# A scan-plus-MLP kernel on one core: a wider on-chip turn, weights decoded in place, and MLP2's weights decoded late

## The chip, the cores and the metric

The kernel runs on one core of a Trainium2 chip. Its time is the device time of one launch in microseconds (us). The kernel before has a median of 1177.3 us in 3 runs (1176.42 to 1181.52).

## What is computed

Three stages on 4 batches of 768 tokens, 8 heads of 40 features (320 in all):

```python
# 1. per head, over t = 0..767: a 40x40 state
y[t] = r[t] @ state
state = state * w[t][:, None] - outer(state @ a[t], b[t]) + outer(v[t], k[t])
# 2. x = y as [768, 320]; token mixing, then a first MLP
h = relu(x.T @ w_tok1) @ w_tok2          # 768 -> 256 -> 768
u = x + h.T
x = u + relu(u @ w_ch1) @ w_ch2          # MLP1: 320 -> 1536 -> 320
# 3. layer norm and a second MLP
out = x + relu(norm(x, g_ln) @ d_ch1) @ d_ch2   # MLP2: 320 -> 1280 -> 320
```

The MLP weights come as 64-bit floats. Every product runs as three f16 matmuls on a high and a low half of each operand.

## The kernel before, in words

**Scan.** Time is cut into chunks of 64 steps, 12 for each batch, 48 in all, taken in 24 pairs. The inputs r, k, v, w, a, b are prepared in six groups G of 8 chunks: `stack` (L778) multiplies an input by running products of w, splits it into f16 halves in the tile `o16` and stores it to a DRAM scratch (`scr_a`, `scr_b`, ...). Later loads read the scratch back, some turned by the DMA. For groups 0 and 1, a and b are also turned on the chip: `turn` (L814) multiplies 32-row slices of `o16` with an identity, 128 matmuls for each input, and ScalarE and VectorE in turn copy eight PSUM banks out (L831, L829). b goes for that time into `d2`, the tile that is later MLP2's second weight. Then come `gram` (L846), and `solve` (L866), 30 dependent steps of two VectorE operations on the tile `ug` (L878, L880), whose result goes to DRAM (`t_d`) and is read by `early` (L996). After that `chain` (L1034) runs each chunk, in order, and `yout_a`, `yout_b` write a batch's x to DRAM (`x_d`).

**Weights.** `decode` (L1150) loads a piece of a weight (up to 384 numbers wide) into a tile `raw`, and four VectorE operations turn the 64-bit floats into 32-bit ones in another tile `wst` (L1155 to L1162). `split` (L1176) scales on ScalarE (L1177), makes the high half on ScalarE (L1180) and the low half on VectorE (L1181). There are 56 pieces: 34 of t1, t2, c1, c1t, c2 and 22 of d1, d1t, d2 (MLP2's weights). `raw` and `wst` are in a pool `boot` that is closed before the pool `moe`, which holds everything of the MLPs, can open in the same memory.

**MLPs.** For each batch, `token_load` reads six tiles xt; `token1` (L1236) makes the hidden token layer in two halves of 160 features, `token2` (L1250) adds the result to xt. `mlp1` (L1319) and `mlp2` (L1330) then work on blocks of 256 tokens, three of each for a batch. In `mlp` (L1296) every 128x512 result is split by ScalarE (L1264) and VectorE (L1265) before the second matmul.

**Order of the work.** All of that is traced in one program order (L1400 to L1440). Then `fix_order` (L543) lists each engine's instructions anew: it plays the program with a table of costs (`cost`, L200) and fixes the order that came out shortest, for PE, DVE, ACT, POOL and the DMA queue on SP. Each engine then runs its list strictly in order, so an instruction that waits holds all behind it. Pools with several buffers add waits: a load into a buffer waits for the last reader of what was there.

Of the kernel before, what the change touches and what calls it, by code (L numbers as in the profile page):

```python
# [200 lines left out]
def cost(i, engine):  # L201
# [351 lines left out]
def tile_main(  # L553
# [47 lines left out]
    WCOL = 384  # L601
# [80 lines left out]
    NA = 8  # L682
# [126 lines left out]
    def t_steps(G):  # L809
# [4 lines left out]
        def turn(n):  # L814
            for i in range(4):
                st = st_i.setdefault(i, {})
                if n == "a":
                    st[n] = stk.tile([128, TU * 128], F16, name="at", bufs=NA)
                    st_t.setdefault(4 * G + i, {})["a"] = st[n]
                else:  # L820
                    st[n] = wt["d2"].rearrange("p m l c -> p (m l c)")[:, i * TU * 128:(i + 1) * TU * 128]
                ls = slice(32 * i, 32 * i + 32)
                for t0 in (0, 16):
                    pt = ps_b.tile([128, 512], F32, name="pb", tag="b")[0:120].rearrange("p (l t) -> p l t", t=16)
                    for t in range(16):
                        nc.tensor.matmul(pt[:, :, t], o16[ls, t0 + t, 0:120], ident[ls, ls], start=True, stop=True)  # L826
                    dst = st[n][0:120].rearrange("p (l t) -> p l t", t=HC)[:, :, t0:t0 + 16]
                    if t0:
                        V.tensor_copy(dst, pt)  # L829
                    else:  # L830
                        A.activation(out=dst, in_=pt, func=ACTF.Copy)  # L831

        def gram_load(i):
            r0 = i * TU * 128
            st = st_i[i] = {}
            st["a"] = stk.tile([128, TU * 128], F16, name="at", bufs=NA)
# [313 lines left out]
    def decode(src, pieces, n):  # L1150
# [4 lines left out]
        V.scalar_tensor_tensor(out=bits[:, 0:n], in0=raw[:, 0:n, 1], scalar=0x38000000, in1=bits[:, 0:n],  # L1155
                               op0=ALU.bitwise_xor, op1=ALU.bitwise_or)
        f = boot.tile([128, WCOL], I32, name="wst", bufs=3)
        V.tensor_scalar(out=f[:, 0:n], in0=raw[:, 0:n, 1], scalar1=0x07FFFFFF, scalar2=3,
                        op0=ALU.bitwise_and, op1=ALU.logical_shift_left)
        nc.vector.scalar_tensor_tensor(out=f[:, 0:n], in0=raw[:, 0:n, 1], scalar=-0x40000000, in1=f[:, 0:n],  # L1160
                                       op0=ALU.bitwise_and, op1=ALU.bitwise_or)
        nc.vector.scalar_tensor_tensor(out=f[:, 0:n], in0=raw[:, 0:n, 0], scalar=29, in1=f[:, 0:n],  # L1162
                                       op0=ALU.logical_shift_right, op1=ALU.bitwise_or)
        return f[:, 0:n].bitcast(F32)
# [3 lines left out]
    def weight_steps():  # L1168
        steps = []

        def cols_of(cols, fn):
            n = cols // -(-cols // WCOL)
            for c0 in range(0, cols, n):
                steps.append(lambda c0=c0: fn(c0, n))

        def split(f, s, hi, lo, p0=0):  # L1176
            A.activation(out=f, in_=f, func=ACTF.Copy, scale=s)  # L1177
            if len(hi.shape) > 2:
                f = by_head(f)
# [3 lines left out]
        def full(name, cols, src, nk, e, gs=None, out=lambda x: x):  # L1183
# [3 lines left out]
            def one(i, c0, n):  # L1187
                f = decode(src, [(0, i * 128, 128, c0)], n)
# [3 lines left out]
            for i in range(nk):  # L1192
                cols_of(cols, lambda c0, n, i=i: one(i, c0, n))
# [293 lines left out]
```

## Time and profile before

| | |
|---|---|
| median of 3 runs | 1177.3 us (1176.42 to 1181.52) |
| profiled execution: time / span | 1180.47 / 1178.8 us |
| PE busy / DVE busy / ACT busy / POOL busy | 904.6 / 770.8 / 507.4 / 206.3 us |
| granted TensorE clock, mean | 0.979 |
| DMA queue of SP | 159.04 MB, 66.6% of 16 engines' span |

PE is TensorE's matmuls, DVE is VectorE, ACT is ScalarE, POOL is GpSimd, SP issues the DMAs. Busy time of an engine is the time in which at least one of its instructions ran; matmuls are pipelined, so their records overlap and the mean of one is longer than the pace at which they follow each other.

### The profile page before, as it was taken

Reading aid. Unit: us, or ns where it says so; the run is one execution under the profiler, and the core shown is the slowest. Engines: PE = TensorE matmul, PEld = TensorE weight load, DVE = VectorE, ACT = ScalarE, POOL = GpSimd, SP = SyncE. Lnnn points to the kernel's source line nnn. Section 1 sums busy time; section 2 is a strip of 40 time slices with the busy share of each in tenths; the row PEclk is TensorE's granted clock in tenths of the full one; section 3 lists DMA queues with packets and bytes.
Section 4 is the critical chain, followed back from the end, with each engine's and each line's share of the span. In section 5 each row is a group of like instructions: output and inputs, shape, how many; then the busy total and the mean of one; then the engine's idle time right before and its main releaser. Section 6 shows DMA issues by size and latency. Waiting matters only on the chain.

```text
span 1178.8 us, 39814 instructions
## 1 busy us (share of the span) xinstructions
PE 904.6 (77%) x17422; PEld 734.4 (62%) x17422; DVE 770.8 (65%) x1936; ACT 507.4 (43%) x1105; POOL 206.3 (17%) x212
## 2 busy tenths in 40 slices
PE   0631450155588878899899999898999999999996
PEld 0620440154577756677677777676777888787774
DVE  6679485868977695657865689656964563443432
ACT  1443333455655453554445545554553343332221
POOL 0235450332000631034120052201000000000000
PEclk9999999999999989989999999999999999999998
DMA  5569826879998778958999757897565532221111
GB/s 159 155 171 242 189 72 193 260 146 182 229 190 162 179 157 198 186 102 160 154 204 162 166 118 170 144 174 173 111 115 93 80 47 47 52 44 21 36 17 26
DMA packets 356903, 161.67 MB, mean 137 GB/s; under 512 B 327536, under 2 KB 336752, under 8 KB 353136
## 3 DMA queue, kind: packets, MB, share of 16 engines
q1 hardware_dynamic: 356720, 159.04, 66.6%
q8 instruction: 138, 2.26, 0.8%
q14 instruction: 45, 0.37, 0.1%
HBM read 71.70 MB, written 50.59 MB: 104 GB/s over the span
## 4 chain that ended last, share of the span: by engine, by line
PE 34%; DVE 8%; DMA 4%; ACT 2%; issue 1%; SPq 1%; POOL 0%; DVEq 0%; ACTq 0%
PE pb L1317 12%; PE pa L1307 9%; PE ch L935 4%; PE pa L1310 3%; PE ps L935 3%; DVE ug L880 1%; DVE hh L1265 1%; PE ps L1014 1%; PE ps L1258 1%; DMA xt<-x_d 1%; DVE tmp L878 1%; DVE u L890 1%; PE ps L993 1%; DMA x<-in_v_dram 1%; DMA x<-in_r_dram 1%
## 5 line engine op out<-in xcount | busy, mean ns | idle before, releaser
L1317 PE MATMUL pb<-c,hh 128*128 128x320 f16 x864 | 179.5, 305 | 2.8 <-ACT hh L1264 2.1
L1317 PEld LDWEIGHTS <-hh 128*128 128x128 f16 x1584 | 153.4, 99 | 39.1 <-ACT hh L1264 3.0
L1265 DVE SCALAR_TENSOR_TENSOR hh<-pa,hh 128x512 f16<-128x512 f32 x132 | 90.6, 687 | 125.8 <-ACT hh L1264 125.3
L1307 PE MATMUL pa<-ut,c 128*128 128x256 f16 x864 | 159.4, 275 | 4.8 <-issue 2.4
L1264 ACT ACTIVATE hh<-pa 128x512 f16<-128x512 f32 x132 | 78.5, 595 | 173.0 <-PE pa L1310 168.2
L1317 PE MATMUL pb<-d,hh 128*128 128x320 f16 x720 | 147.6, 301 | 0.9 <-ACT hh L1264 0.7
L1307 PE MATMUL pa<-ut,d 128*128 128x256 f16 x720 | 137.7, 279 | 9.1 <-DVE hh L1265 6.2
L1307 PEld LDWEIGHTS <-c 128*128 128x128 f16 x864 | 83.4, 99 | 25.7 <-issue 5.3
L1307 PEld LDWEIGHTS <-d 128*128 128x128 f16 x720 | 69.8, 100 | 25.8 <-issue 8.2
L795 ACT ACTIVATE o<-x 128x2560 f16<-128x2560 f32 x30 | 69.9, 2331 | 20.9 <-DMA x<-in_a_dram 7.2
L880 DVE TENSOR_TENSOR ug<-ug,tmp 128x30 f32<-128x30 f32 (+9 forms) x180 | 73.0, 405 | 1.4
L878 DVE TENSOR_TENSOR tmp<-ug 128x30 f32<-128x30 f32 (+9 forms) x180 | 69.5, 386 | 4.2 <-POOL ug L872 2.6
L1343 POOL TENSOR_TENSOR y<-ve,mhalf 128x2 f32<-128x2 f32 x12 | 8.9, 741 | 353.3 <-DVE stats L1339 214.6
L826 PE MATMUL pb<-ident,o 32*120 32x32 f16 x512 | 50.3, 283 | 23.8 <-POOL o L797 13.2
L1310 PE MATMUL pa<-ut,c1t 128*128 128x256 f16 x288 | 65.4, 276 | 0.0
L826 PEld LDWEIGHTS <-o 32*120 32x120 f16 x512 | 49.1, 214 | 24.7 <-POOL o L797 13.4
L797 POOL TENSOR_TENSOR o<-x,o 128x1280 f16<-128x1280 f32 x15 | 49.7, 3314 | 59.2 <-ACT o L795 40.3
L935 PEld LDWEIGHTS <-srx 64*64 64x64 f16 x2304 | 51.8, 122 | 10.8 <-issue 8.1
L1310 PE MATMUL pa<-ut,d1t 128*128 128x256 f16 x240 | 55.5, 277 | 0.0
L858 PE MATMUL pa<-at,d 120*32 120x32 f16 (+1 forms) x384 | 5.2, 206 | 63.9 <-DVE lc L862 61.3
L935 PE MATMUL ch<-vx,sak 64*64 64x40 f16 x1152 | 33.9, 198 | 26.4 <-DVE n L1087 16.7
L722 POOL TENSOR_TENSOR x<-x,sx 128x1280 f32<-128x1280 f32 x10 | 33.1, 3307 | 115.7 <-DMA x<-in_k_dram 63.5
(204 smaller groups left out, 1914.2 us busy)
## 6 DMA issues: line engine op xcount, KB each, us to landing
raw<-in_moe_w_ch_dram SPq DMA_DIRECT2D x30, 320.0 KB
scr_b<-o SPq DMA_DIRECT2D x6, 1024.0 KB
scr_k<-o SPq DMA_DIRECT2D x6, 1024.0 KB
scr_v<-o SPq DMA_DIRECT2D x6, 1024.0 KB
scr_r<-o SPq DMA_DIRECT2D x6, 1024.0 KB
t_d<-u SPq DMA_DIRECT2D x24, 256.0 KB
tu<-t_d SPq DMA_DIRECT2D x24, 256.0 KB
scr_a<-o SPq DMA_DIRECT2D x4, 1024.0 KB
```

Of the source, the lines that this page charges most:

```text
L722: eng.tensor_tensor(out=o, in0=x, in1=y, op=ALU.mult)
L795: A.activation(out=hi2, in_=x.unsqueeze(2).broadcast_to([128, HC, 2, D]), func=ACTF.Copy, scale=p2(e))
L797: P.tensor_tensor(out=o16[:, :, lo:lo + D], in0=x, in1=o16[:, :, 0:D], op=ALU.subtract)
L826: nc.tensor.matmul(pt[:, :, t], o16[ls, t0 + t, 0:120], ident[ls, ls], start=True, stop=True)
L878: V.tensor_tensor(out=tv, in0=ug[:, 0:s, s:s + 1].broadcast_to([128, s, n]), in1=ug[:, s:s + 1, s + 1:32].broadcast_to([128, s, n]), op=AL ...
L880: V.tensor_tensor(out=ug[:, 0:s, s + 1:32], in0=ug[:, 0:s, s + 1:32], in1=tv, op=ALU.add)
L935: m = nc.tensor.matmul(out, lhsT, rhs, start=start, stop=stop, skip_group_check=True)
L1264: nc.scalar.activation(out=hi, in_=ps, func=ACTF.Relu)
L1265: nc.vector.scalar_tensor_tensor(out=lo, in0=ps, scalar=0.0, in1=hi, op0=ALU.max, op1=ALU.subtract)
L1307: nc.tensor.matmul(o, w1[:, f, l, ms], ut[:, f + 3 * q, :], start=n == 0, stop=False)
L1310: nc.tensor.matmul(o, w1t[:, ms], ut[:, 2 + 3 * q, :], start=False, stop=q == 1)
L1317: nc.tensor.matmul(pb[i][:, 0:DM], hh[:, l, c0:c0 + 128], w2[:, m0 + s, q, :], start=m0 + s == 0 and n == 0, stop=m0 + s == nm - 1 and n == 2)
```

## The change

Five edits, and the engines' orders that follow from them:

1. `turn` works on all 128 rows of `o16` at once: 32 matmuls of 128x128 (32 pieces of time, output step 4 floats) for an input in place of 128 of 32x32 (output step 16 floats). Still eight banks are copied out.
2. `decode` works in place in `raw` (four buffers, no `wst`), with the same number of VectorE operations; `split` puts the scale into the two operations that make the halves, so ScalarE's separate scaling goes. Tiles whose columns are regrouped by head (c2, d2) are split in two halves.
3. d1, d1t and d2 are no longer decoded before `moe` opens but traced after it (`run(wlate)`), 160 numbers wide in 44 pieces in place of 22, in four tiles borrowed from the rings xt and xn of `moe`.
4. The token layer of batch 0 is made in one walk (`wide`) of full 320 columns, in both `pa` banks.
5. Batch 0 runs its three MLP1 blocks, then MLP2 (before: MLP1 0, MLP1 1, MLP2 0, MLP1 2, MLP2 1). The planner's cost for a PE output with a step is at least 100 ns.

```diff
 def cost(i, engine):
+        if i.outs[0].ap[-1][0] > 1:
+            return max(100, t), 0
 def turn(n):
-                ls = slice(32 * i, 32 * i + 32)
-                for t0 in (0, 16):
-                    for t in range(16):
-                        nc.tensor.matmul(pt[:, :, t], o16[ls, t0 + t, 0:120], ident[ls, ls], start=True, stop=True)
+            for t0 in range(0, HC, 4):
+                pt = ps_b.tile([128, 512], F32, name="pb", tag="b")[0:120].rearrange("p (l t) -> p l t", t=4)
+                for t in range(4):
+                    nc.tensor.matmul(pt[:, :, t], o16[:, t0 + t, 0:120], ident, start=True, stop=True)
+                if t0 % 8:
+                    V.tensor_copy(dst[:, :, t0:t0 + 4], pt)
+                else:
+                    A.activation(out=dst[:, :, t0:t0 + 4], in_=pt, func=ACTF.Copy)
 def decode(src, pieces, n, raw=None):
-        raw = boot.tile([128, WCOL, 2], I32, name="raw", bufs=3)
+        if raw is None:
+            raw = boot.tile([128, WCOL, 2], I32, name="raw", bufs=4)
...
-        f = boot.tile([128, WCOL], I32, name="wst", bufs=3)
+        lo, hi = raw[:, 0:n, 0], raw[:, 0:n, 1]
+        V.tensor_scalar(out=lo, in0=lo, scalar1=29, scalar2=-0x40000000,
+                        op0=ALU.logical_shift_right, op1=ALU.bitwise_xor)
+        V.scalar_tensor_tensor(out=lo, in0=hi, scalar=3, in1=lo,
+                               op0=ALU.logical_shift_left, op1=ALU.bitwise_xor)
+        V.scalar_tensor_tensor(out=lo, in0=hi, scalar=-0x80000000, in1=lo,
+                               op0=ALU.bitwise_and, op1=ALU.bitwise_or)
+        def slot():
+            if not slots_d:
+                for name in ("xt", "xt", "xn", "xn"):
+                    t = moe.tile([128, DM], F32, name=name, bufs=8 if name == "xt" else 2)
+                    slots_d.append(t.bitcast(I32).rearrange("p (c w) -> p c w", w=2))
+            slots_d.append(slots_d.pop(0))
+            return slots_d[-1]
 def split(f, s, hi, lo, p0=0):
-            A.activation(out=f, in_=f, func=ACTF.Copy, scale=s)
...
-            A.activation(out=hi, in_=f, func=ACTF.Copy)
-            V.tensor_tensor(out=lo, in0=f[p0:128], in1=hi[p0:128], op=ALU.subtract)
+            A.activation(out=hi, in_=f, func=ACTF.Copy, scale=s)
+            V.scalar_tensor_tensor(out=lo, in0=f[p0:128], scalar=s if isinstance(s, float) else s[p0:128],
+                                   in1=hi[p0:128], op0=ALU.mult, op1=ALU.subtract)
+    def wide(bb):
+        ps = [token_bank(bb) for _ in range(NJ)]
+        for i in range(NT):
...
+                    nc.tensor.matmul(ps[jt][:, 0:DM], wt["t1"][:, i, l, jt * 128:(jt + 1) * 128], o[:, m, :],
+                                     start=i == 0 and n == 0, stop=i == NT - 1 and n == 2)
 def moe_body(bb):
+        if bb == 0:
+            return ([lambda k=k: mlp1(bb, k) for k in range(NBK)]
+                    + [lambda k=k: mlp2(bb, k) for k in range(NBK - 1)])
...
     run(wtodo)
     late.close()
     moe = late.enter_context(tc.tile_pool(name="moe", bufs=2))
+    attend(0, 4)
+    run(bg(2))
+    attend(4, 8)
+    run(wlate)
```

Three places of the engines' lists that the steps below use. The first is DVE at the turn of b of group 1, beside the solve of group 0 (`ug` and `tmp` are the solve's, `d2_181` takes the turned b, `pb` are its PSUM banks, `raw`, `wst`, `bits` belong to the decoding of weights). Before:

```order
L829 CAST d2_181<-pb_1006 120x32x16
L878 TENSOR_TENSOR tmp_841<-ug_829 128x84
L829 CAST d2_181<-pb_1042 120x32x16
L880 TENSOR_TENSOR ug_829<-ug_829,tmp_841 128x3x28
L1160 SCALAR_TENSOR_TENSOR wst_1864<-raw_1860,wst_1864 128x384
L878 TENSOR_TENSOR tmp_844<-ug_829 128x108
L829 CAST d2_181<-pb_1078 120x32x16
```

Now:

```order
L831 CAST d2_181<-pb_799 120x128x4
L1198 SCALAR_TENSOR_TENSOR c1t_170<-raw_1430,c1t_170 64x384
L831 CAST d2_181<-pb_811 120x128x4
L882 TENSOR_TENSOR tmp_640<-ug_634 128x30
L1167 SCALAR_TENSOR_TENSOR raw_1439<-raw_1439 128x384
L831 CAST d2_181<-pb_823 120x128x4
```

The copies of the turn still stand among the solve's steps and the decoding; the solve now begins between them.

The second is DVE at the start of batch 0's first MLP1 block (`hh` are the splits of its hidden layer; `xn_6516`, `xn_6515` and the like are now borrowed tiles with late weights). Before:

```order
L878 TENSOR_TENSOR tmp_4893<-ug_4803 128x58
L1265 SCALAR_TENSOR_TENSOR hh_7824<-pa_7807,hh_7824 128x512
L880 TENSOR_TENSOR ug_4803<-ug_4803,tmp_4893 128x29x2
L878 TENSOR_TENSOR tmp_4896<-ug_4803 128x30
L880 TENSOR_TENSOR ug_4803<-ug_4803,tmp_4896 128x30
L1265 SCALAR_TENSOR_TENSOR hh_7856<-pa_7839,hh_7856 128x512
```

Now:

```order
L1306 SCALAR_TENSOR_TENSOR hh_7466<-pa_7449,hh_7466 128x512
L884 TENSOR_TENSOR ug_4139<-ug_4139,tmp_4172 128x10x21
L1194 SCALAR_TENSOR_TENSOR d2_181<-xn_6516,d2_181 128x80
L882 TENSOR_TENSOR tmp_4175<-ug_4139 128x220
L1306 SCALAR_TENSOR_TENSOR hh_7498<-pa_7481,hh_7498 128x512
L884 TENSOR_TENSOR ug_4139<-ug_4139,tmp_4175 128x11x20
L1194 SCALAR_TENSOR_TENSOR d2_181<-xn_6516,d2_181 128x80
L882 TENSOR_TENSOR tmp_4178<-ug_4139 128x228
L1163 TENSOR_SCALAR xn_6515<-xn_6515 128x160
```

The block's splits, which stood beside the last steps of the solve of group 2, now stand beside its middle, with late weights between.

The third is SP while the chains of batch 0 run (`kt`, `vt`, `rt`, `kb`, `yw`, `tu` are loads for the chains, `raw`, then `xt` and `xn` with `in_moe_w_ch`, are weights). Before:

```order
L957 DMA kb<-scr_b_129 128x8x80
L966 DMA yw<-scr_y_132 128x8x40
L1146 DMA x_d_3062<-yo 64x2x160 x2
L1153 DMA raw<-in_moe_w_ch_dram 128x640 x2
L957 DMA vx<-scr_v_130 128x8x80
L864 DMA l_d_141<-sab 128x8x32
```

Now:

```order
L958 DMA_TRANSPOSE kt<-scr_k_128 128x1024
L1257 DMA xt<-x_d_2401 128x320
L1158 DMA xt<-in_moe_w_ch_dram 64x320 x2
L1158 DMA xn<-in_moe_w_ch_dram 64x320 x2
L1158 DMA xt<-in_moe_w_ch_dram 64x320 x2
L958 DMA_TRANSPOSE rt<-scr_r_131 128x1024
```

The weight loads in this stretch are narrower and more of them stand between the loads for the chains.

## Rows read from the trace of the kernel before

**Rows 1.** The page: span, and busy time of each engine.
```profile
span 1178.8 us, 39814 instructions
PE 904.6 (77%) x17422; PEld 734.4 (62%) x17422; DVE 770.8 (65%) x1936; ACT 507.4 (43%) x1105; POOL 206.3 (17%) x212
```

**Rows 2.** Stretches of the span: busy time by engine, clock, DMA share, GB/s.
```profile
0.00:198.00 198.00, 60.79 (x932) 58.36 (x933) 134.01 (x304) 67.28 (x114) 68.02 (x79) 1.00 0.64 164
...
198.00:441.00 243.00, 154.01 (x4099) 130.69 (x4099) 197.93 (x476) 132.81 (x303) 57.85 (x45) 0.99 0.92 192
441.00:470.00 29.00, 25.87 (x329) 19.81 (x327) 16.04 (x42) 11.60 (x22) 5.28 (x8) 0.94 0.86 189
470.00:612.00 142.00, 128.24 (x2591) 98.77 (x2590) 98.43 (x253) 69.68 (x147) 35.97 (x40) 0.93 0.93 160
612.00:1179.00 567.00, 535.65 (x9478) 426.75 (x9476) 324.43 (x865) 225.98 (x520) 39.15 (x40) 0.98 0.51 96
```

**Rows 3.** Timeline of DVE: solve of group 0, first step and end, its stall.
```profile
120.99 0.19 DVE L878 TENSOR_TENSOR tmp<-ug 128x30 f32<-128x30 f32 x1 [2.63 <-POOL ug L872]
...
189.71 0.33 DVE L1158 TENSOR_SCALAR wst<-raw 128x320 int32<-128x320 int32 x1 [13.75 <-DMA raw<-in_moe_w_ch_dram]
...
198.27 0.20 DVE L880 TENSOR_TENSOR ug<-ug,tmp 128x30 f32<-128x30 f32 x1
```

**Rows 4.** What DVE waited for, 0 to 200: total, times, longest.
```profile
DVE wst L1158 <- DMA raw<-in_moe_w_ch_dram: 25.1, 6, 13.7
DVE d L829 <- PE pb L826: 14.9, 8, 3.1
DVE at L829 <- PE pb L826: 7.0, 5, 2.0
```

**Rows 5.** Timeline of PE: one turn of a; four 128x128 transposes.
```profile
52.88 11.89 PE L826 MATMUL pb<-ident,o 32*120 32x32 f16 x128 [4.79 <-DVE o L799]
...
359.76 0.61 PE L1116 MATMUL pb<-ident,n 128*128 128x128 f16 x4
```

**Rows 6.** The turn's copies out of PSUM, by line: min/median/max ns.
```profile
L829 DVE CAST d<-pb x8: 691/692/692, 37.5 to 140.8; 120x512 f16<-120x512 f32 x8
...
L831 ACT ACTIVATE d<-pb x8: 597/597/598, 35.9 to 139.2; 120x512 f16<-120x512 f32 x8
```

**Rows 7.** Groups by line and shape: busy, mean ns, idle before.
```profile
L878 DVE TENSOR_TENSOR tmp<-ug 128x30 f32<-128x30 f32 (+9 forms) x180 | 69.5, 386 | 4.2 <-POOL ug L872 2.6
L880 DVE TENSOR_TENSOR ug<-ug,tmp 128x30 f32<-128x30 f32 (+9 forms) x180 | 73.0, 405 | 1.4
L1162 DVE SCALAR_TENSOR_TENSOR wst<-raw,wst 128x320 int32<-128x320 int32 x34 | 18.0, 531 | 0.2
L1076 DVE SCALAR_TENSOR_TENSOR sas<-ch,sas 128x160 f16<-128x160 f32 x48 | 15.3, 318 | 12.6 <-ACT sas L1075 12.4
L1158 DVE TENSOR_SCALAR wst<-raw 128x320 int32<-128x320 int32 x34 | 11.3, 333 | 16.2 <-DMA raw<-in_moe_w_ch_dram 16.0
L1177 ACT ACTIVATE wst<-wst 128x320 f32<-128x320 f32 x22 | 10.2, 464 | 24.5 <-DVE wst L1162 24.4
L1181 DVE TENSOR_TENSOR d<-wst,d 128x320 f16<-128x320 f32 x18 | 8.7, 484 | 0.2
```

**Rows 8.** Timeline of DVE: token2's last write; first MLP1 block's write.
```profile
441.10 0.48 DVE L1260 SCALAR_TENSOR_TENSOR xt<-pa,xt 128x320 f32<-128x320 f32 x1
...
469.64 0.98 DVE L1327 SCALAR_TENSOR_TENSOR xt<-pb,xt 128x320 f32<-128x320 f32 x2 [2.10 <-PE pb L1317]
```

**Rows 9.** SP: issue of weight loads, ns; its waits, 198 to 440.
```profile
L1153 SPq DMA_DIRECT2D raw<-in_moe_w_ch_dram x54: 322/518/3505, 53.5 to 358.5; - x54
...
SPq L1153 <- DVE wst L1162: 6.8, 8, 1.5
SPq L1153 <- DVE ch L1085: 6.2, 1, 6.2
```

**Rows 10.** Timeline of POOL: the split that ran slowest.
```profile
167.26 11.17 POOL L797 TENSOR_TENSOR o<-x,o 128x1280 f16<-128x1280 f32 x1 [14.08 <-ACT o L795]
```

More of the change, by code (lines that the diff above doesn't have):

```diff
@@ L1148, in tile_main, with decode @@
     wt = {}
-    def decode(src, pieces, n):
-        raw = boot.tile([128, WCOL, 2], I32, name="raw", bufs=3)
+    def decode(src, pieces, n, raw=None):
+        if raw is None:
+            raw = boot.tile([128, WCOL, 2], I32, name="raw", bufs=4)
         for p0, r0, np_, c0 in pieces:
@@ L1173, in cols_of @@
+        def cols_of(cols, fn, late=False):
+            n = DCOL if late else cols // -(-cols // WCOL)
             for c0 in range(0, cols, n):
                 steps.append(lambda c0=c0: fn(c0, n))
+        def slot():
[5 more added lines that the diff above has]
+            return slots_d[-1]
@@ L1176, in split @@
         def split(f, s, hi, lo, p0=0):
-            A.activation(out=f, in_=f, func=ACTF.Copy, scale=s)
             if len(hi.shape) > 2:
-                f = by_head(f)
-            A.activation(out=hi, in_=f, func=ACTF.Copy)
-            V.tensor_tensor(out=lo, in0=f[p0:128], in1=hi[p0:128], op=ALU.subtract)
-        def full(name, cols, src, nk, e, gs=None, out=lambda x: x):
+                f, k = by_head(f), f.shape[-1] // 80
+                for h in range(2):
+                    A.activation(out=hi[:, :, h], in_=f[:, :, h], func=ACTF.Copy, scale=s)
+                    V.scalar_tensor_tensor(out=lo[:, :, h], in0=f[:, :, h], scalar=s, in1=hi[:, :, h],
+                                           op0=ALU.mult, op1=ALU.subtract)
@@ L1184, in full @@
+                return
+            A.activation(out=hi, in_=f, func=ACTF.Copy, scale=s)
+            V.scalar_tensor_tensor(out=lo, in0=f[p0:128], scalar=s if isinstance(s, float) else s[p0:128],
+                                   in1=hi[p0:128], op0=ALU.mult, op1=ALU.subtract)
+        def full(name, cols, src, nk, e, gs=None, out=None):
             src = src.bitcast(I32)
@@ L1187, in one @@
             def one(i, c0, n):
-                f = decode(src, [(0, i * 128, 128, c0)], n)
+                f = decode(src, [(0, i * 128, 128, c0)], n, slot() if name[0] == "d" else None)
                 s = p2(e) if gs is None else gs[:, i:i + 1]
-                split(f, s, out(o[:, i, 0, c0:c0 + n]), out(o[:, i, 1, c0:c0 + n]))
+                if out is by_half:
+                    hi, lo = (by_half(o[:, i, q])[:, c0 // 80:(c0 + n) // 80] for q in range(2))
+                else:
+                    hi, lo = (o[:, i, q, c0:c0 + n] for q in range(2))
+                split(f, s, hi, lo)
             for i in range(nk):
-                cols_of(cols, lambda c0, n, i=i: one(i, c0, n))
+                cols_of(cols, lambda c0, n, i=i: one(i, c0, n), name[0] == "d")
         def tail(name, cols, src, e, gs=None):
@@ L1218, in weight_steps @@
         V.tensor_scalar(out=gs2, in0=gs, scalar1=p2(E_D1), scalar2=None, op0=ALU.mult)
+        n_early = len(steps)
         full("d1", DC2, d_ch1, 2, E_D1, gs2)
@@ L1221, in weight_steps @@
         full("d2", DM, d_ch2, M2, E_D2, out=by_half)
-        return steps
+        return steps[:n_early], steps[n_early:]
     h16 = {}
@@ L1238, in token1 @@
             h16[bb] = moe.tile([128, NJ, 2, DM], F16, name="h16", bufs=1)
+        if bb == 0:
+            if z == 0:
+                wide(bb)
+            return
         n0 = DM // 2
@@ L1251, in token1 @@
         relu_split(ps, h16[bb][:, :, 0, cs], h16[bb][:, :, 1, cs])
+    def wide(bb):
+        ps = [token_bank(bb) for _ in range(NJ)]
+        for i in range(NT):
+            x, o = x_t[bb][i], moe.tile([128, 2, DM], F16, name="x16", tag="u16", bufs=2)
+            nc.scalar.activation(out=o[:, 0, :], in_=x, func=ACTF.Copy, scale=p2(E_X))
+            nc.vector.scalar_tensor_tensor(out=o[:, 1, :], in0=x, scalar=p2(E_X),
+                                           in1=o[:, 0, :], op0=ALU.mult, op1=ALU.subtract)
+            for jt in range(NJ):
+                for n, (l, m) in enumerate(T3):
+                    nc.tensor.matmul(ps[jt][:, 0:DM], wt["t1"][:, i, l, jt * 128:(jt + 1) * 128], o[:, m, :],
+                                     start=i == 0 and n == 0, stop=i == NT - 1 and n == 2)
+        for jt in range(NJ):
+            relu_split(ps[jt][:, 0:DM], h16[bb][:, jt, 0], h16[bb][:, jt, 1])
     def token2(bb, i):
@@ L1423, in tile_main @@
     V.tensor_scalar(out=cnt[:, 0:1], in0=cnt[:, 0:1], scalar1=0.0, scalar2=None, op0=ALU.is_equal)
-    attend(0, 4)
-    run(bg(2))
-    attend(4, 8)
     run(moe_head(0))
```

47 lines of the change are left out of this document (19 added, 28 removed).

## Prediction

> **What bounds the kernel now.** The page's first part [rows 1] says only that no engine is full over the whole span: PE 77%, DVE 65%. The view by stretches [rows 2] says where each is. From 612 us to the end PE is busy 535.65 of 567 us, and from 470 to 612 it is busy 128.24 of 142: from the first MLP work on, PE is the bound, and what DVE does there lies beside it. From 198 to 441 us DVE is busy 197.93 of 243 us and PE 154.01: the chains of batch 0 run here, each engine's list is in order, and DVE is the nearest to full. From 0 to 198 us nothing is full (DVE 134.01, PE 60.79): this stretch is made of waits. Its end is the end of group 0's solve, for which the chains wait, and the solve shows the waits best [rows 3]: it runs from 120.99 to 198.47 us, 77 us for work of 30 × (0.386 + 0.405) = 23.7 us [rows 7]. Between its steps DVE copies out the turned b and a of group 1 and decodes weights. The list of DVE's waits [rows 4] names both: 14.9 + 7.0 = 21.9 us for the turn's matmuls (four turns) and 25.1 us for weight loads.
>
> So the change is worth what it moves the start of the PE-bound part, and costs what it adds to DVE and SP ahead of that start. From 612 us on PE's list has the same chains and blocks in the same order as before, so that stretch is taken as unchanged.
>
> **The turn.** 128 matmuls take 11.89 us [rows 5], 0.093 each. Now there are 32. Their price is not in the trace: a 128x128 output with a step of 4 floats. Lower end: the transposes with the same 128 columns follow each other at (0.61 - 0.31)/3 = 0.10 us, if the last record lasts 0.31 [rows 5], so 3.2 us a turn. Upper end: the old matmul wrote 32 columns with a wider step in 0.093 us, so a column costs no more than 2.9 ns, 128 columns 0.37 us, and a turn stays at 11.9 us. I take 0.10, the transpose being the nearest in shape. Then the copies set the pace: eight of 0.60 (ACT) and 0.69 (DVE) [rows 6], two banks, each going round in 0.4 + 0.69 us plus two hand-overs, put at 0.2 together: four rounds, 5 to 6 us. A turn gains 6 us.
>
> Group 0's two turns stand in a row on the way to the solve: 12 us. What follows them waits for loads that the turn does not hasten (the 25.1 us of rows 4), so I count half, 6. Group 1's two stand beside the solve, where DVE waits for them in order: about half of the 21.9 us, of which some 2.5 stay: 8.5. **Sum -14.5 us**; ends 0 (upper price) and -24 (all four in full).
>
> **The decoding.** A piece of 320 costs DVE 0.333 + 3 × 0.50 + 0.484 = 2.3 us (L1158, three like L1162, whose group mean is 0.531 with the slower ones in it, and L1181) [rows 7]; the 22 pieces of MLP2 are 51 us, all ahead of 441 us. Late they are 44 of 160 numbers: three operations and the split at 0.318 (the row of a 160-wide one, L1076) and a TENSOR_SCALAR put at 0.2, 1.5 us a piece, 66 us: the edit adds 15 us to DVE. DVE's list shows that they hardly leave the way of the chains: 32 of the 44 still stand ahead of token2's last write, 48 us for 51. **-3 us.** What does leave is group 2's solve: of its 30 steps 23 stood ahead of that write and now 6, so 17 × 0.79 = **-13 us**. With DVE at 81% in this stretch I count both in full; ends -4 and -20.
>
> The in-place TENSOR_SCALAR now also writes with a step of two numbers. With a stepped input it does 320 in 333 ns, against 531 for an operation with two inputs [rows 7]; at that second pace 78 pieces would cost up to 10 us more. I take the first. The Trainium skill (VectorE: DVE Perf Modes, section What auto-detection actually checks) grants a one-source operation with source and destination in SBUF the double rate by even outer dimensions, without asking for a step of one; by that the +10 us falls away.
>
> Both sides of the stretch are counted: those 17 solve steps (13 us) and five late pieces (7.5 us) now stand in batch 0's first MLP1 block. That block ran from 441.10 to 469.64 us [rows 8] with 16.04 us of DVE [rows 2]; now 37 us of DVE stand there in order with the block's splits, so PE waits for DVE. At a load between 81% and 100% it takes 37 to 46 us; I take 41. **+12 us**, ends +8 and +17.
>
> From there to 612 us eight more late pieces, 12 us, join 98.43 us of DVE in 142 [rows 2]: 110, less than PE's 128. **0**, at worst +12.
>
> **Costed at nothing.** ScalarE loses 50 scalings of about 0.46 us [rows 7]; it is busy 43% [rows 1] and on no long wait, so hidden. The wide walk streams the same columns, half the weight loads, in a stretch bound by DVE. MLP1 three times, then MLP2: the same PE work. Fourth `raw` buffer: see the second rival. SP gets 26 more weight loads (90 for 64) at a median of 0.518 us [rows 9], 13 us of issue between 200 and 500 us; hidden as long as the loads for the chains behind them are issued early enough. That cover is the first rival.
>
> **Sum:** -14.5 - 3 - 13 + 12 = -18.5 us. The profiled execution took 1180.5 us (span 1178.8), so 1162; the median of the runs shown is 3.2 us below the profiled one: **1159 us**.
>
> **Rivals.**
> *Slower: the borrowed tiles hold up SP.* A load into one of the four tiles waits on SP until DVE and ACT have read the last piece, and behind it stand the transposing loads of k, v, r for the chains. Before, weight loads held SP for 6.8 and 6.2 us in this stretch [rows 9]. With twice as many such waits (+13) and 26 issues (+13) all passed on to the chains, the sum is -18.5 + 26 = +8: 1185 us. It decides from 0.7 us for each of the 26 added loads (18.5/26). For it: DMA share 0.92 and a list in order; against it: DVE waited for weights mostly ahead of 198 us, and the slots rotate over four tiles. The Trainium skill (DMA: Bandwidth & Descriptors, section Rules for kernel authors) speaks against this edit too: many small transfers should be joined into one. This trace has no row of these loads at half size.
>
> *More: the head's load waits go as well.* The 13.75 us stall in the solve [rows 3] came because SP stood at a load that waited for the POOL split of 11.17 us [rows 10], with the weight loads behind it. Four `raw` buffers and another list could remove it: -18.5 - 13.7 = -32, 1145 us. Against it: the list still has the same POOL split beside solve and decoding.
>
> *Nothing: the turn does not get faster.* At the upper price the turn gives nothing and the rest is -4: 1173 us, no change. For it: no row has that output step at this width.
>
> **Chances and range.** A measurement of this kernel can tell about 0.5%, 6 us. Forecast (1150 to 1171) 0.52; more 0.18; nothing 0.14; slower 0.16. So faster 0.70, same 0.14, slower 0.16. Below, the range takes in the second rival with the full price of all four turns: 1159 - 13.7 - 9.5 = 1136, put at 1135. Above it holds the third rival and the milder half of the first: 1180. The forecast alone has 1150 to 1171.
>
> **What would show it.** Right: a turn of 32 matmuls in 5 to 7 us with DVE's waits for it below 10 us in all; group 0's solve ending near 184 us instead of 198; token2's last write near 410 us instead of 441; the first MLP1 block longer, some 41 us for 28.5, with PE waiting for DVE; the stretch from there to the end as before. Wrong: turns still near 12 us; DVE waiting for late weights after 200 us; SP's waits in front of weight loads above 20 us there; or a PE less busy after the first block than 94%, which would mean that the added 15 us of DVE are no longer beside PE.

## The result, and the profile after

The changed kernel took **1161.0 us** (median of 5 runs, 1151.3 to 1163.6), the kernel before in the same measurement 1176.4 us: ratio **0.985, 95% interval 0.980 to 0.990**. A second measurement, below, gave 0.981 (0.978 to 0.985). The prediction was 1159 us and faster. The sign and the size came out; the way there did not, as the experiments show.

One caution for all that follows. The profiled execution of the changed kernel took 1151.3 us, 10 us under its median; that of the kernel before took 1180.5 us, 4 us over its five-run median. So the two profiles lie 29 us apart where the medians lie 15. The second profile of the changed kernel (1161.4 us, span 1159.7) is a typical one, and sizes are read there where they matter; it is called the second profile.

The page, first profile, answering to [rows 1]:

```profile
span 1149.6 us, 39204 instructions
PE 877.6 (76%) x17002; PEld 704.6 (61%) x17002; DVE 774.3 (67%) x2072; ACT 491.8 (43%) x1097; POOL 203.6 (18%) x212
```

PE has 27 us less (the turn alone went from 50.3 us in 512 matmuls to 24.7 in 128), ACT 16 less (the scalings), DVE 3.5 more.

The timeline of DVE, first profile, answering to [rows 3, 8]: first and last step of group 0's solve, token2's last write of batch 0, last write of its first MLP1 block.

```profile
117.32 0.19 DVE L882 TENSOR_TENSOR tmp<-ug 128x30 f32<-128x30 f32 x1
...
173.04 0.21 DVE L884 TENSOR_TENSOR ug<-ug,tmp 128x30 f32<-128x30 f32 x1
...
396.94 0.49 DVE L1301 SCALAR_TENSOR_TENSOR xt<-pa,xt 128x320 f32<-128x320 f32 x1
...
431.28 0.47 DVE L1368 SCALAR_TENSOR_TENSOR xt<-pb,xt 128x320 f32<-128x320 f32 x1
```

The head came out shorter than predicted: the solve ends at 173 us (predicted 184, before 198.3), token2's last write stands at 396.9 (predicted 410, before 441.1). The second profile has 176.7 and 399.8:

```profile
399.80 0.48 DVE L1301 SCALAR_TENSOR_TENSOR xt<-pa,xt 128x320 f32<-128x320 f32 x1
```

DVE's waits from 0 to 200 us, first profile, answering to [rows 4] (total, times, longest):

```profile
DVE raw L1163 <- DMA raw<-in_moe_w_ch_dram: 18.3, 4, 6.6
...
DVE at L831 <- PE pb L829: 5.2, 2, 4.5
DVE d L831 <- PE pb L829: 2.8, 4, 1.0
```

The waits for the turn fell from 21.9 to 8.0 us, those for weights from 25.1 to 18.3.

Now the part that the prediction had as unchanged. Stretches of the second profile, from batch 0's first block on (columns as in [rows 2]):

```profile
400.00:435.00 35.00, 31.60 (x440) 24.66 (x440) 33.42 (x108) 17.58 (x46) 6.09 (x2) 0.95 1.01 206
435.00:600.00 165.00, 147.17 (x2832) 114.11 (x2831) 122.36 (x319) 80.43 (x175) 41.57 (x48) 0.92 0.83 163
600.00:700.00 100.00, 80.72 (x2004) 66.36 (x2003) 68.60 (x175) 46.46 (x117) 18.91 (x25) 0.80 0.77 148
```

and of the kernel before:

```profile
600.00:700.00 100.00, 93.86 (x2163) 72.81 (x2162) 64.83 (x164) 51.82 (x121) 19.40 (x28) 0.98 0.87 154
```

Between 600 and 700 us PE now idles 19.3 us where it idled 6.1, and the granted clock there is 0.80 for 0.98. Batch 0's MLP blocks are used up at 602.7 us (before: 669.2), batch 1's token walk starts at 641, and between them PE has only the scan's work (the chains, and what prepares the next ones). From 602 to 642 us the granted clock is 0.53, so mostly the lower of the two levels. The same 24 matmuls of a chain take 0.83 us in that hole and 0.56 us after it:

```profile
619.73 0.83 PE L939 MATMUL ch<-vx,sak 64*64 64x40 f16 x24 [0.94 <-DVE n L1091]
...
662.57 0.56 PE L939 MATMUL ch<-vx,sak 64*64 64x40 f16 x24 [0.71 <-DVE n L1091]
```

So of the 41 us won at token2's last write (441.1 to 399.8) 19 were left at the end (spans 1178.8 and 1159.7). What the lower clock has in that was not tested. An estimate: PE is busy for 24.4 us from 602 to 642 us, and at the pace of the later row it would be 24.4 × 0.56 / 0.83 = 16.5, so the clock can account for at most some 8 us.

### The profile page after: what moved, and what is told of

It reads as the page before. It is cut to its first block, busy times and chain, and to the rows that moved or that the text cites. A ratio compares the mean times of both kernels' runs of the same rounds, so it can differ in the third digit from the quotient of the medians.

```text
span 1149.6 us, 39204 instructions
## 1 busy us (share of the span) xinstructions
PE 877.6 (76%) x17002; PEld 704.6 (61%) x17002; DVE 774.3 (67%) x2072; ACT 491.8 (43%) x1097; POOL 203.6 (18%) x212
## 4 chain that ended last, share of the span: by engine, by line
PE 53%; DVE 19%; DMA 14%; ACT 5%; issue 4%; SPq 2%; POOL 1%; ACTq 0%; DVEq 0%; POOLq 0%
PE pb L1358 15%; PE pa L1348 12%; PE ch L939 8%; PE ps L939 5%; PE pa L1351 4%; DMA x<-in_v_dram 3%; PE ps L1018 2%; ACT o L797 2%; DVE tmp L882 2%; PE pb L939 2%; DVE ug L884 2%; DMA raw<-in_moe_w_ch_dram 2%; DMA raw<-in_moe_w_tok_dram 1%; DMA x<-in_r_dram 1%; PE ps L997 1%
## 5 line engine op out<-in xcount | busy, mean ns | idle before, releaser
L1358 PE MATMUL pb<-c,hh 128*128 128x320 f16 x864 | 174.7, 303 | 0.0
L1358 PE MATMUL pb<-d,hh 128*128 128x320 f16 x720 | 142.6, 299 | 1.1 <-DVE hh L1306 1.1
L1348 PE MATMUL pa<-ut,d 128*128 128x256 f16 x720 | 132.8, 275 | 2.0 <-DVE hh L1306 2.0
L882 DVE TENSOR_TENSOR tmp<-ug 128x30 f32<-128x30 f32 (+9 forms) x180 | 77.0, 428 | 1.0
L939 PEld LDWEIGHTS <-kb 64*40 64x40 f16 x2112 | 42.4, 103 | 20.2 <-issue 18.1
L799 POOL TENSOR_TENSOR o<-x,o 128x1280 f16<-128x1280 f32 x15 | 45.2, 3013 | 50.8 <-ACT o L797 30.3
L724 POOL TENSOR_TENSOR sx<-sx 128x40 f32<-128x40 f32 (+2 forms) x50 | 25.0, 509 | 163.6 <-DVE sx L750 162.1
L939 PE MATMUL ch<-vx,sak 64*64 64x40 f16 x1152 | 33.7, 198 | 24.7 <-DMA vx<-scr_v 12.0
L981 DVE TENSOR_TENSOR ps<-ps,causal 128x512 f32<-128x512 f32 x60 | 41.5, 694 | 15.0 <-PE ps L997 14.8
L939 PEld LDWEIGHTS <-sak 64*64 64x64 f16 x1152 | 28.2, 125 | 31.7 <-DVE n L1091 13.1
```

The source lines that it names most:

```text
L724: eng.tensor_tensor(out=o, in0=x, in1=y, op=ALU.mult)
L799: P.tensor_tensor(out=o16[:, :, lo:lo + D], in0=x, in1=o16[:, :, 0:D], op=ALU.subtract)
L882: V.tensor_tensor(out=tv, in0=ug[:, 0:s, s:s + 1].broadcast_to([128, s, n]), in1=ug[:, s:s + 1, s + 1:32].broadcast_to([128, s, n]), op=AL ...
L939: m = nc.tensor.matmul(out, lhsT, rhs, start=start, stop=stop, skip_group_check=True)
L981: V.tensor_tensor(out=sm, in0=sm, in1=causal.unsqueeze(1).broadcast_to([128, 8, 64]), op=ALU.mult)
L1348: nc.tensor.matmul(o, w1[:, f, l, ms], ut[:, f + 3 * q, :], start=n == 0, stop=False)
```

## The experiments

All ratios are to the kernel before on the same chip, whose median was 1172.9 to 1178.5 us in the four groups; ratios, not times, are compared across groups.

| kernel | ratio | 95% interval |
|---|---|---|
| turn only | 0.994 | 0.990 to 0.998 |
| decoding in place only | 0.986 | 0.982 to 0.990 |
| both of these | 0.992 | 0.989 to 0.995 |
| change, old turn | 0.996 | 0.992 to 0.999 |
| change, MLP2's weights early | 0.988 | 0.985 to 0.991 |
| change, old order of blocks | 0.990 | 0.986 to 0.994 |
| change, two half walks | 0.986 | 0.982 to 0.990 |
| change, again | 0.981 | 0.978 to 0.985 |
| change, second order of the planner | 0.994 | 0.992 to 0.996 |
| before, second order | 0.992 | 0.989 to 0.994 |
| before, third order | 0.996 | 0.993 to 0.999 |
| change, last MLP2 block held back | 0.998 | 0.995 to 1.001 |

**First group: the edits one by one.** The turn alone: `turn` and the planner's cost rule put into the kernel before.

```diff
-                        nc.tensor.matmul(pt[:, :, t], o16[ls, t0 + t, 0:120], ident[ls, ls], start=True, stop=True)
+                    nc.tensor.matmul(pt[:, :, t], o16[:, t0 + t, 0:120], ident, start=True, stop=True)
```

> The kernel before with the wider turn alone. My theory (the turn is worth 14.5 us by itself): 1176.4 - 14.5 = 1162 us, a turn of 32 matmuls in about 6 us, and group 0's solve ends near 184 us where it ended at 198.3. Rival (what follows the turn waits for loads anyway, so the turn gives little alone; the changed kernel's gain came from the decoding): 1172 us or more, and the solve ends after 192 us.

Measured: 1167.0 us against 1173.4, half of what I expected; the solve ends at 189.2 us, between the two theories. The other way round, the changed kernel with the old lines:

> The changed kernel with the narrow turn of 128 matmuls put back, all else kept. My theory: it loses the 14.5 us again, 1161 + 14.5 = 1175 us, and group 0's solve ends some 14 us or more after the 173.0 us of the changed kernel. Rival (the decoding carries the gain): at most 1166 us.

Measured: 1169.4 us against 1173.4, ratio 0.996. Against the change's 0.981 to 0.985 that is 12 to 17 us lost, about twice what the turn gains alone. One edit, two values: this does not fit a sum of terms. And the sign that I had named did not come: group 0's solve ends 5 us before the 173.0 of the change, not 14 us after it, so what was lost was not lost at that solve.

```profile
167.99 0.20 DVE L880 TENSOR_TENSOR ug<-ug,tmp 128x30 f32<-128x30 f32 x1
```

MLP2's weights decoded with the others:

```diff
-    run(wtodo)
+    run(wtodo + wlate)
...
-    run(wlate)
```

(and the slots and the width of 160 left out for them).

> The changed kernel with MLP2's weights decoded with the others, before the MLPs' pool opens, in 22 full-width pieces in place of 44 narrow ones. My theory (late decoding is worth -3 - 13 + 12 = -4 us): 1165 us; token2's last write of batch 0 some 16 us after the 396.9 us of the changed kernel, the first MLP1 block back from 34 to about 29 us. Rival (the head is short because these 51 us of VectorE are out of it; of the 44 us at token2 the turn explains at most 24): 1175 us or more, token2's last write after 417 us.

Measured: 1159.5 us against 1173.4, ratio 0.988. The landmarks moved as my theory has it: token2's last write is 14 us later than in the second profile, and the block after it takes 27 us (413.81 to 440.8) in place of 35. The end cannot be told apart: the ratio is 0.3 to 0.7% above the change's, 3 to 8 us, where my theory said 4, but the other orders below move the time by more than that with no edit; and its profiled execution, the fastest of its six runs, took 1152.6 us, between the two of the change (1151.3 and 1161.4).

```profile
413.81 0.48 DVE L1301 SCALAR_TENSOR_TENSOR xt<-pa,xt 128x320 f32<-128x320 f32 x1
```

Batch 0's blocks in the old order:

```diff
-        if bb == 0:
-            return ([lambda k=k: mlp1(bb, k) for k in range(NBK)]
-                    + [lambda k=k: mlp2(bb, k) for k in range(NBK - 1)])
```

> The changed kernel with batch 0's blocks in the old order (MLP1 0, MLP1 1, MLP2 0, MLP1 2, MLP2 1). My theory (the order is worth nothing, the same PE work in a stretch where PE is full): within 6 us of the changed kernel's 1161 us. Rival (the new order is what gives the late pieces their time: the first MLP2 matmul stood at 511.1 us, and it would stand one block, about 40 us, earlier, when the last late weight loads, at 453 us, have just been decoded): 5 to 15 us slower, with PE waiting for late weights ahead of the first MLP2 block.

Measured: 1162.3 us against 1173.4, ratio 0.990. That is 0.5 to 0.8% above the change, 5 to 10 us, which does not tell the two theories apart by itself. The rival's wait is not there: PE's longest wait from 400 to 560 us is 7.9 us for a split of the hidden layer (6.8 in the second profile of the change), none is for a late weight.

**Second group: the unplaced rest.** The kernel before with the decoding in place alone (`decode`, `split`, `full` and `tail` of the change, all pieces early):

```diff
-        f = boot.tile([128, WCOL], I32, name="wst", bufs=3)
+        lo, hi = raw[:, 0:n, 0], raw[:, 0:n, 1]
```

> The kernel before with the decoding in place (four buffers for raw, scale folded into the halves) as its only edit; all weights decoded early, narrow turn, two half walks, old order. So far the turn is worth about 7 us, the late decoding and the order about nothing, and 5 to 6 of the 13 to 15 us are not yet placed. Theory A (a fourth buffer and ScalarE's missing step let the pieces flow, which I had costed at nothing): 1168 us against 1173.4 of the kernel before, with less than the 25.1 us that VectorE waited for raw ahead of 200 us. Theory B (the wide walk has them): 1171 to 1175 us.

Measured: 1164.6 us against 1178.5, ratio 0.986: an edit that I had costed at nothing gives nearly what the whole change gives. DVE's waits for `raw` ahead of 200 us fall from 25.1 to 13.1, as theory A says, and the turn's waits (11.7 and 7.1) are still there:

```profile
DVE raw L1159 <- DMA raw<-in_moe_w_ch_dram: 13.1, 5, 7.4
```

But this does not show theory A. The kernel before in its second order, with no edit (third group below), waits even less there:

```profile
DVE wst L1158 <- DMA raw<-in_moe_w_ch_dram: 9.1, 5, 2.5
```

The change with two half walks in batch 0:

```diff
-        if bb == 0:
-            if z == 0:
-                wide(bb)
-            return
```

> The changed kernel with batch 0's token layer in two half walks again. Theory A (the in-place decoding has the missing 5 to 6 us; the walk streams the same columns): within 3 us of the changed kernel, 1158 to 1164 us. Theory B (the wide walk has them, since VectorE and ScalarE split six wide tiles in place of twelve half ones and PE waits for them once): 1165 to 1168 us, with a longer way from the last chain of batch 0 to token2's last write.

Measured: 1161.9 us against 1178.5, ratio 0.986. Token2's last write now stands at 419.8, 20 us later than with the wide walk, and the spans of the two profiled executions are 1160.3 and 1159.7.

```profile
419.82 0.48 DVE L1297 SCALAR_TENSOR_TENSOR xt<-pa,xt 128x320 f32<-128x320 f32 x1
```

So 20 us at the landmark on which my sum was built are worth 0.6 us at the end of these two profiles, and 0 to 0.4% in the medians.

The change itself, once more, gives the other end of its range:

> The changed kernel itself, to stand beside its variants with as many runs as they have: 1155 to 1163 us, ratio 0.98 to 0.992. Were it 1165 us or more, the variants with late decoding undone and with the old order would beat it.

Measured: 1157.8 us against 1178.5, ratio 0.981.

**Third group: the order as a suspect.** Every edit makes the planner find new lists for all engines. It makes eleven complete orders and keeps the shortest by its own table of costs. These kernels do the same work in another order:

```diff
-    best = g.schedule(g.urgency())
+    plans = [g.schedule(g.urgency())]
     for _ in range(ROUNDS):
-        trial = g.schedule(g.latest(g.finish))
-        best = min(best, trial, key=lambda t: t[0])
+        plans.append(g.schedule(g.latest(g.finish)))
+    best = sorted(plans, key=lambda t: t[0])[1]
```

> The kernel before, the same instructions, with the planner's second shortest of its eleven orders in place of the shortest. If the order is worth what the edits are worth (theory: each edit brings a new order, and part of what it shows is that order), this differs from the kernel before by 5 us or more, in either sign. Rival (the orders are equally good, and the 16 us of the in-place decoding alone are its own): within 3 us of the kernel before.

Measured: 1167.0 us against 1177.2, ratio 0.992: **10 us faster with no edit at all.** The third order ([2] in place of [1]), run in the last group:

> The kernel before, the same instructions, with the planner's third shortest order. If the kernel before was shown with a poor order (theory: most of the change's measured gain is that its order came out better), this one is near the second: ratio 0.988 to 0.996. Rival (the second order was a lucky one, and the change's gain is its edits'): 0.997 to 1.003.

Measured: 1167.8 us against 1172.9, ratio 0.996. And the change with its second order:

> The changed kernel, the same instructions, with the planner's second shortest order. Theory (the order decides part): 5 us or more away from the changed kernel's ratio of 0.983, that is below 0.979 or above 0.987; the hole of TensorE at 602 to 642 us, 16 to 19 us of idle time between 600 and 700, is of another size. Rival: ratio 0.981 to 0.986.

Measured: 1168.5 us against 1177.2, ratio 0.994: 10 to 15 us of the change's gain are gone with no edit undone. With second orders on both sides, the changed kernel (1168.5) and the kernel before (1167.0) take the same time, although the change keeps its shorter head. Group 0's solve ends at 166.6 us in the one and at 196.7 in the other:

```profile
166.62 0.20 DVE L884 TENSOR_TENSOR ug<-ug,tmp 128x30 f32<-128x30 f32 x1
```

```profile
196.73 0.20 DVE L880 TENSOR_TENSOR ug<-ug,tmp 128x30 f32<-128x30 f32 x1
```

So what an order is worth is as large as what the edits are worth, and a kernel with one edit more or less is also another draw of the order. The two first edits together show it again:

> The kernel before with two of the edits, the wider turn and the decoding in place; all weights early, half walks, old order. If the edits' worths add (alone they had ratios 0.9938 and 0.9862): 0.980, 1155 us where the kernel before has 1178.5, better than the changed kernel. If both shorten the same wait in the head, or the single values were those of lucky orders: 0.984 to 0.990, 1160 to 1167 us.

Measured: 1167.0 us against 1177.2, ratio 0.992: slower than the in-place decoding alone (0.986). Adding the turn cost 0.5% here, gave 0.6% in the first kernel of this study and 1.0 to 1.4% inside the change. One worth of the turn that adds to the other edits' cannot be all three. That its worth depends on the other edits is not ruled out by these runs, but the spread of the orders is enough to explain it.

**Fourth group: an attempt at a better version.** PE's idle time after 602 us looked like the place where the head's gain is given back. Batch 0's last MLP2 block was held on PE until chain 24 had run, so that it stands beside chains 25 to 28 (`begun[24]` is that chain's last matmul of its third part):

```diff
+        begun[g] = acc.since[0][-1]
...
+                        if hold is not None:
+                            after(mm, begun[hold])
+                            hold = None
```

> The changed kernel, with batch 0's last MLP2 block held behind chain 24 on TensorE, so that it stands beside the chains that ran alone from 602 to 642 us. Theory (that hole gives back some 10 us of what the head gained: 16.3 and 19.3 us of idle TensorE between 600 and 700 us where the kernel before has 6.1): idle time there down to 6 to 10 us, ratio about 0.974, 1147 us where the kernel before has 1177. Rival (a new order is another draw, and the idle time moves elsewhere): ratio 0.981 to 0.994.

Measured: 1170.2 us against 1172.9, ratio 0.998: 1.3 to 1.7% slower than the change. Its stretches, and what PE waited for longest from 600 to 700 us:

```profile
500.00:600.00 100.00, 75.14 (x1291) 56.27 (x1288) 61.31 (x157) 39.60 (x76) 20.86 (x16) 0.84 0.75 146
600.00:700.00 100.00, 86.39 (x2046) 68.87 (x2047) 70.19 (x173) 46.80 (x118) 26.17 (x34) 0.87 0.75 148
```

```profile
PE ps L863 <- DMA tt_b<-scr_b: 14.0, 1, 14.0
```

In the second profile of the change the same wait is its longest there, too:

```profile
PE ps L862 <- DMA tt_b<-scr_b: 5.1, 1, 5.1
```

The idle time from 600 to 700 us fell from 19.3 to 13.6, but from 500 to 600 it is now 24.9 (4.5 in the second profile of the change). The sum grew, and the order of all engines is another one again. So filling the hole did not help: it is where the lack of ready work shows. Chain 25 came 4 us earlier (620.6 for 624.8), chain 28 not at all, and the gram of group 4 stood 14 us on PE, up to 603 us, for the load of its turned b. My theory of the hole fell with this run. What keeps the chains there was not settled. The waits point to the preparation of the next groups. One of them: SP stood 13.4 us, up to 543 us, at the load of an input whose buffer a split on POOL was still reading, with the store and the turning loads of group 4 behind it in its list.

How little the head moves the chains behind the hole is shown by one write (`r` of chain 28, L1070, L1074 or L1076) in four kernels: the kernel before, its second order, the change (second profile), and the held one.

```profile
661.55 0.31 DVE L1070 SCALAR_TENSOR_TENSOR r<-ch,r 128x160 f16<-128x160 f32 x1
```

```profile
658.98 0.32 DVE L1070 SCALAR_TENSOR_TENSOR r<-ch,r 128x160 f16<-128x160 f32 x1
```

```profile
657.14 0.32 DVE L1074 SCALAR_TENSOR_TENSOR r<-ch,r 128x160 f16<-128x160 f32 x1
```

```profile
657.16 0.32 DVE L1076 SCALAR_TENSOR_TENSOR r<-ch,r 128x160 f16<-128x160 f32 x1
```

Token2's last write in these four stands at 441.1, 425.2, 399.8 and 393.7: 47 us apart. Chain 28 is 4.4 us apart. Over the 14 profiles of all kernels here it stands between 646.0 (turn only) and 662.9 us (old order of blocks), and not earlier where token2 is earlier: the turn alone has token2 at 419.8 us, the held kernel at 393.7 and its chain 28 at 657.2.

One chain later the rest differs less from kernel to kernel. From the `r` of chain 29 to the end there are 488 to 500 us in the 14 profiles, from token2's last write 737 to 773. Chain 29 in the kernel before, the change (second profile) and the held one:

```profile
682.00 0.33 DVE L1070 SCALAR_TENSOR_TENSOR r<-ch,r 128x160 f16<-128x160 f32 x1
```

```profile
666.27 0.32 DVE L1074 SCALAR_TENSOR_TENSOR r<-ch,r 128x160 f16<-128x160 f32 x1
```

```profile
667.40 0.32 DVE L1076 SCALAR_TENSOR_TENSOR r<-ch,r 128x160 f16<-128x160 f32 x1
```

This was read afterwards, and a later point has less left to vary, so it places the loss without naming its cause: 41 us at token2, 16 at chain 29, 19 at the end.

**What the edits are worth, as far as it goes.** Taking every ratio as one draw (the change at 0.983, the mean of its two; the held kernel left out): the seven kernels with the new turn have a mean of 0.989, the five with the old one 0.994. The eight with the decoding in place have 0.989, the four without 0.995. Among the eight, late decoding has 0.990 and early decoding 0.989. So some 5 us for the turn, some 7 for the decoding in place, nothing for the late decoding. Single kernels of one kind spread by 0.8 to 1.1%, and most kernels with the new turn also decode in place: a fit of both values to the twelve ratios at once leaves 2.5 us for the turn and 6 for the decoding, each with a standard error of 3 us. So the turn's own worth is not shown, and the decoding's is not clear of the noise. No kernel was faster than the change as it was given.

## Why the prediction was right, and where it was not

**The turn as such: right in size.** The four turns take 7.0, 6.9, 7.4 and 8.9 us where one took 11.9 [rows 5]; here are the first turn of b and the two ends of the last turn of a on PE, first profile.

```profile
31.45 5.38 PE L829 MATMUL pb<-ident,o 128*120 128x128 f16 x28 [5.37 <-DVE o L801]
37.81 0.60 PE L829 MATMUL pb<-ident,o 128*120 128x128 f16 x4 [0.99 <-DVE d L831]
...
132.42 4.56 PE L829 MATMUL pb<-ident,o 128*120 128x128 f16 x20 [13.10 <-POOL o L799]
...
140.27 1.01 PE L829 MATMUL pb<-ident,o 128*120 128x128 f16 x4 [0.34 <-DVE at L831]
```

The price of 0.10 us for a matmul holds at one level of the clock only. Two rows of eight matmuls with no stop between them, in the third turn, and the stretches that they stand in (the number after POOL is the granted clock):

```profile
111.97 1.96 PE L829 MATMUL pb<-ident,o 128*120 128x128 f16 x8
...
117.34 1.03 PE L829 MATMUL pb<-ident,o 128*120 128x128 f16 x8 [0.35 <-DVE d L831]
```

```profile
111.90:114.00 2.10, 2.10 (x12) 1.68 (x9) 1.22 (x4) 0.89 (x2) 0.98 (x1) 0.50 1.11 355
117.30:118.40 1.10, 1.03 (x8) 0.90 (x8) 1.08 (x3) 0.72 (x2) 0.00 (x0) 1.00 1.08 452
```

With records of 0.50 and 0.31 us that is (1.96 - 0.50) / 7 = 0.21 us a matmul at the lower level and (1.03 - 0.31) / 7 = 0.10 at the higher. The plain transposes from which I took 0.10 [rows 5] cost that at the lower level: in the second profile four of them take the same 0.61 us with a granted clock of 0.50.

```profile
636.31 0.61 PE L1120 MATMUL ps<-ident,n 128*128 128x128 f16 x4
```

So at one level the stepped matmul costs twice the plain one (that the step does it is the nearest reading, not tested). At the lower level 32 of them would take 6.7 us, an estimate, more than the 5 to 6 us that I had from the copies. At the higher one PE stops for the copies as I had it: 0.99 us ahead of the last four of the first turn. The rival that the turn is not faster is out. DVE's waits for it are 8.0 us, below the 10 I named. **Its worth, -14.5, is a term that was mis-sized:** alone it brought the end of group 0's solve forward by 9 us (198.3 to 189.2) and the kernel's by 6.4, and the fit over all kernels leaves less. What the head gains does not all reach the end.

**The decoding: both signs right, no effect shown.** The predicted -16 us at token2's last write measured 14 (413.8 to 399.8, early against late), the predicted +12 in the block behind it measured 8 (27 to 35 us). Their sum should have been worth 4 us, which these runs cannot tell from nothing. One price in it was off. The late pieces' operations, second profile:

```profile
L1161 DVE SCALAR_TENSOR_TENSOR bits<-xn,bits 128x160 int32<-128x160 int32 x22 | 8.8, 399 | 0.0
...
L1163 DVE TENSOR_SCALAR xn<-xn 128x160 int32<-128x160 int32 x22 | 8.3, 376 | 2.4 <-DMA xn<-in_moe_w_ch_dram 2.3
...
L1194 DVE SCALAR_TENSOR_TENSOR d<-xn,d 128x80 f16<-128x80 f32 x20 | 5.7, 310 | 0.4 <-ACT d L1193 0.3
...
L1163 DVE TENSOR_SCALAR raw<-raw 128x320 int32<-128x320 int32 x12 | 3.8, 320 | 7.3 <-DMA raw<-in_moe_w_ch_dram 7.2
```

A narrow TENSOR_SCALAR takes 0.376 us in the mean (0.236 in the median, with single ones up to 2.7) where I put 0.2, and a piece of d2 has two splits of 0.31 (its columns are regrouped by head) where I counted one: a piece costs 1.8 to 2.0 us, not 1.5, and all 44 about 81 us, not 66. The wide in-place one takes 0.320 us for 320 numbers, with an output step of two numbers now, against 0.333 before [rows 7]: the possible +10 us did not come, as the rule drawn from the Trainium skill (VectorE: DVE Perf Modes, section What auto-detection actually checks) had it.

**"Costed at nothing": wrong for the decoding in place.** The fourth `raw` buffer and the missing scaling on ScalarE alone gave 0.986. I had looked only at ScalarE's share and at its long waits, and had the buffer in a rival. How much of that is the order is open; 6 to 7 us seem the edit's own, with the error given above. The wide walk, also costed at nothing, brings token2 20 us forward, and of that 0 to 0.4% of the time is left at the end: right in the sum, for a reason that I had not given. (The scalings that go are 56, one for each piece, not 50; nothing hangs on it.)

**The step that failed** is the frame of the sum: "the change is worth what it moves the start of the PE-bound part", with 0 for the time from there to 612 us, and after it "that stretch is taken as unchanged". The two kernels do not have the same work there: the kernel before still runs batch 0's MLP2 until 669 us, the change has none of it after 603. And 19.3 us of idle PE between 600 and 700 us (6.1 before) stand against it. I named a PE below 94% after the first block as a sign of being wrong; in the first profile, from 431.3 us on, it is 664.8 of 718.3 us, 92.6%, and before, from 470.1 us on, 663.8 of 708.7, 93.7%. The sign fired, but it was set badly: the kernel before is under 94% as well. What it shows is the difference, 53.5 us of idle PE against 44.9. The reason that I had tied to it, the added work on DVE, is a part: from 431 to 600 us PE waits 8.4 us for DVE's splits (second profile; 2.4 and 0.7 before), 6.8 of them at 453 us, where the splits of group 2's solved tile, a split of an input that waited for ScalarE and a late piece stand ahead of one of them:

```profile
PE pa L1348 <- DVE hh L1306: 8.4, 3, 6.8
```

The larger part, from 600 to 700, is not: there PE waits longest for a load of the next group (5.1 us), and chain 28 does not come earlier with the head. So the stretch from which the rest is as before begins near chain 29, not at token2. What was read as one bound was two: PE is full, but with blocks that could go elsewhere, while the chains have a pace of their own. What sets that pace stays open.

**Why the total still came out.** By errors that cancel, which is luck. In the second profile token2 gained 41 us where I expected 31, the first block gave back 6 where I expected 12, and 16 more went after it where I expected 0. The remaining 19 us of the profiles (15 of the medians) are near my 18.5. And part of them may be the order alone: the kernel before, as given, is the slowest of its three orders, and the change, as given, the faster of its two. On equal terms (three orders against two) the means are 0.996 and 0.989, so about 8 us, with an uncertainty of some 7 (an estimate from the spread of these orders). That the change as given is faster than the kernel as given is measured; that its edits are, whatever the order, is not shown.

**The rivals.** *SP held up by the borrowed tiles:* no. SP waited ahead of the weight loads, second profile, 198 to 480 us:

```profile
SPq L1158 <- DVE bits L1161: 8.6, 2, 8.0
SPq L1158 <- DVE d L1198: 8.5, 2, 7.3
```

With 19.8 us in other waits that is 36.9 us (19.5 in the kernel before), above the 20 that I gave as a sign of being wrong, and DVE waited 7.9 us for late weights in the first profile, another sign that I had named. Yet the kernel with early decoding, with no narrow loads and 17.0 us of such waits, is not faster: the price was there, and nothing of it is seen at the end. *The head's load waits go too:* in part (25.1 to 18.3 us); the second order of the kernel before has 9.1 with no edit, so this wait follows the order.

## What to carry to other kernels

Where a planner lays out all engines anew for each edit, an edit is measured together with a draw of the order. Measure a few orders of the same instructions first: here they differ by 10 us, and less than that cannot be put down to an edit by one kernel with it and one without. A landmark in the middle is no proxy for the end unless an experiment has moved it alone; here one moved by 20 us and the end by 0.6. A landmark is of use where the time from it to the end is the same in many kernels: here 488 to 500 us from chain 29, but 737 to 773 from token2.

## Unexpected on the chip: the recorded clock

The stretch 200 to 390 us, kernel before and change, first profiles (the number after POOL is the granted clock):

```profile
200.00:390.00 190.00, 111.82 (x3406) 98.55 (x3405) 155.32 (x375) 104.71 (x240) 36.35 (x30) 1.00 0.95 193
```

```profile
200.00:390.00 190.00, 138.70 (x3679) 113.33 (x3679) 143.44 (x400) 97.76 (x234) 41.20 (x40) 0.53 0.89 173
```

By these numbers the change halved the clock (1.00 is 2.4 GHz, 0.50 is 1.2), which would make it a cost of the shorter turn. But the trace of the kernel before has no clock record ahead of 427.1 us, where the first one is a rise, and the view counts a stretch without a record as 1.00. The matmuls show what the clock was. The same group (line of the chain's products, 64x40) in that stretch, before and after, and then the kernel before at 700 to 900 us, where 0.98 is recorded:

```profile
L935 PE MATMUL pb<-kb,srx 64*64 64x40 f16 x576 | 19.8, 219 | 2.4 <-issue 1.3 <-ACT nmt L1118 1.0
```

```profile
L939 PE MATMUL pb<-kb,srx 64*64 64x40 f16 x576 | 19.5, 219 | 2.8 <-ACT nmt L1122 2.6
```

```profile
L935 PE MATMUL ps<-kb,srx 64*64 64x40 f16 x576 | 12.7, 184 | 0.0
```

219 ns in both heads, 184 later: both ran this stretch at the lower level, and the 1.00 shown for the kernel before is not borne out. The mean of 0.979 in the table of the kernel before is too high for the same reason; an estimate with 0.50 up to 427 us gives 0.80, beside 0.825 for the change. In the five kernels with the old turn the first clock record is a rise at 291 to 427 us, in the nine with the new one a rise at 32 to 45 us, in the change at 34.4, after its first wide matmuls (from 31.45 us on). The Trainium skill (TensorE: Matmul & The Clock Gate, section Seeing it yourself) warns that such clock events can be unreliable; the trace agrees. A granted clock is to be read beside the duration of one and the same matmul.
